# One core, attention, expert mixing and a gated feed-forward: an opening in another order and new step times

## The chip, the cores and the metric

The kernel runs on one core of one Trainium2 chip. The metric is the device time of one launch in microseconds (us); lower is better. The engines are PE (TensorE: matmuls and transposes, with PEld for its weight loads), DVE (VectorE), ACT (ScalarE), POOL (GpSimd) and SP (SyncE), whose queue issues nearly all transfers between DRAM and on-chip memory.

## What is computed

Three layers, one after the other, on 8 batches of 576 tokens with 512 features. Shortened from the reference:

```python
def sm_attn(qq, kk, vv):                 # softmax(scale * qq kk^T) vv
    ...
p_packed = sm_attn(p, k, v)              # 32 packed queries per head, 8 heads
x = sm_attn(q, p_packed, p_packed)       # 576 queries against the 32 packed rows
...
logits = x @ w_gate                      # 4 experts, the best 2 are kept
for e in range(4):
    q, k, v = x @ wq[e], x @ wk[e], x @ wv[e]
    a = softmax(causal(scale * q @ k.T))
    out += weight[e] * (a @ v @ wo[e])
...
x_prev = shift_by_one_token(x)
xk, xr = mu_k * x + (1 - mu_k) * x_prev, mu_r * x + (1 - mu_r) * x_prev
k = np.maximum(xk @ w_k, 0.0)
return sigmoid(xr @ w_r) * (k * k @ w_v)
```

The weights w_k, w_r and w_v arrive as 64-bit floats.

## The kernel before

The work is written as Python generators, one per piece, and each `yield` ends a step. Every step has a number on one time axis (20 units a batch, `U`), and the steps are traced in the order of these numbers. A list scheduler then orders the instructions of each engine, by readiness in its own model and by a priority that a step may carry. What runs on the chip is that fixed order: each engine takes its instructions one after the other and waits where an operand is not there. The constants at the top of the file are the step numbers and priorities.

The pieces that matter here:

- `front(b, g)` is the first attention of batch b for the head group g (two groups of four heads). Its chain is: scores `s1` on PE from `kT` and `pT` (by `eight`), row maximum `mx` on DVE, exp into `a` on ACT, transposes on PE, `aT` on ACT, times `vn` on PE, `pp` on DVE (L291), a transpose on PE (L296), `ppT` on ACT, scores `s2` with `qT` on PE, `st` on DVE (L303), maximum, difference (L308), exp, then `wa` times `ppT` on PE, whose result is split into a rounded part `PWh` (ACT) and a rest `PWl` (DVE, L315); at last `a2` (DVE) with its parts `A2h` and `A2l` (L329). For batch 0 the small steps of this chain run on DVE, later on POOL.
- `values` and `project` multiply `PW` and `A2` on PE into `vg` and into q and k of two experts; two swaps `qs` and `ks` by DMA move halves of them between partitions (L428, L429). `soft`, `turn` and `pair_out` are the second attention: scores (L466), maximum on DVE (L478), exp on ACT (L482), transposes (L505, L512), `tb` on ACT, times `vg` on PE (L548), scaling, and `dt` on POOL, stored to `dscr` (L582).
- `fold` is weight work of no batch: it loads `won` and splits it on POOL into `woTh` and `woTl` (L202, L646), then for each of 24 blocks of w_k and w_r fetches `raw` (128 x 512 words, 256 KB), decodes it (`decode`: `dce`, `dcx`, `dce`, `dcu` on DVE, `dcx` on POOL at L626, `dcq` on ACT, `wc` on DVE at L640), splits it on POOL and multiplies it on PE (L695) into DRAM. It is spread over the attention in 57 steps (`FOLD_T`).
- Behind the attention come the R stage (`rstage`, L854: six blocks of 256 token groups, two halves each; `load_block` fetches `dl` in four parts per block, two blocks fit), the K stage (L874) and the V stage (L915). `swap_w` and `load_weight` bring `wr`, and `swap_end` brings `wk0` and `wk1` (four transfers of 512 KB each) for them.

The transfers of the opening, in SP's order before: pT 64 KB, kT 576, pT 64, kT 576, vn 512 and 64, qT 576 (group 0), vn 512 and 64, qT 576 (group 1), wa 2 x 772, won 512, raw 256, raw 256. Tiles for matmul results are few: two `big` ones and four `one` ones on the chip's accumulator memory.

Of the kernel before, what the change touches and what calls it, by code (L numbers as in the profile page):

```python
# [22 lines left out]

FRONT_T = [-29.55, -25.88, -23.33, -18.77, -17.51, -15.03, -12.67, -12.1, -8.35]
G1_T = [1.16, 2.9, 3.77, 1.72, 1.63, 2.21, 3.77, 1.1, 3.2]
VAL_T = [-2.9, -1.08, -0.99, -0.13, 0.58]
PROJ_T = [-2.12, -1.5, 1.92, 2.48]
GROUPS = ((0, 3), (1, 2), (4,))
SOFT_T = [1.36, 2.42, 3.15]
TURN_LAG = [4.11, 4.87, 5.4]  # L30
OUT_LAG = [3.85, 4.64, 7.81]
FOLD_T = [-20.0, 10.15, 107.63]
FOLD_N = 13
WA_AT = -28.3
PR0, WARM = (1000, 1000, 1000, 1000, 1000, 1000, 940, 980, 980), 16
WR_AT = 6.87
R_LOAD, R_RUN = ([14.0, 15.0], [22.0, 28.0])
W_AT = [1.69, 3.59]
K_AT = [(0, -1.0, 0)] + [(0, 0.0, j) for j in range(4)] + [(1, -1.0, 0)] + [(1, 0.0, j) for j in range(5)]
# [8 lines left out]
E_DT, E_WL = "P", "P"  # L48
PR = {'front': 0, 'values': -100, 'project': 0, 'soft': 0, 'turn': 0, 'out': 100, 'fold': 0, 'k': 0, 'gates': 0}


def f32(ap):
    return ap.bitcast(F32)
# [3 lines left out]
def kernel(  # L57
# [5 lines left out]
    P = 128  # L63
# [77 lines left out]
    if True:  # L141
# [59 lines left out]
        def pool_copy(o, x):  # L201
            nc.gpsimd.tensor_scalar(o, x, 1.0, 0.0, op0=ALU.mult, op1=ALU.add)  # L202

        def evac(eng, o, x):
            if eng == "A":
                nc.scalar.copy(o, x)  # L206
            elif eng == "V":
                nc.vector.tensor_copy(o, x)
            else:
                pool_copy(o, x)  # L210

# [18 lines left out]
        def load(b, gs):  # L230

            for g in gs:
                pT = pTs[(b * NG + g) % 2]
                nc.sync.dma_start(pT, p[b, g].rearrange("d j n -> d (j n)"))
                kT = ld.tile([P, NH, SH], F32, tag="kT", name=nm("kT"))
                nc.sync.dma_start(kT, k[b, g])
                loaded[b, g] = [pT, kT]
            for g in gs:
                vn = vns[(b * NG + g) % 2]
                nc.sync.dma_start(  # L240
                    vn[:, : NT - 1, :], v[b, g, : (NT - 1) * P].rearrange("(c p) x -> p c x", p=P)
                )
                nc.sync.dma_start(vn[TAIL:, NT - 1, :], v[b, g, (NT - 1) * P :])
                qT = ld.tile([P, NH, SH], F32, tag="qT", name=nm("qT"))
                nc.sync.dma_start(qT, q[b, g])
                loaded[b, g] += [vn, qT]

        def front(b, g):
# [33 lines left out]
            for c in range(NT):  # L282
# [7 lines left out]
            pp = fr.tile([P, 2, D], F32, tag="pp", name=nm("pp"))  # L290
            nc.vector.tensor_scalar(  # L291
                pp, ps[:, :D].unsqueeze(1).to_broadcast([P, 2, D]), ri, None, op0=ALU.mult
            )
            yield
            ps = one()
            nc.tensor.transpose(ps[:, :P], pp.rearrange("p x d -> p (x d)"), ident)  # L296
            ppT = fr.tile([P, P], F32, tag="ppT", name=nm("ppT"))
            evac(E_PPT, ppT, ps[:, :P])
# [354 lines left out]
        def fold():  # L655

            won = dv.tile([P, NDT, 2 * P], F32, tag="wc", name=nm("won"), bufs=1)
            nc.sync.dma_start(won, wo.rearrange("(c p) n -> p c n", p=P))  # L660
            woT = {x: dv.tile([P, NDT, 2 * P], F32R, name="woT" + x, bufs=1) for x in "hl"}
# [428 lines left out]
```

## Time and profile before

| | |
|---|---|
| median of 3 runs | 827.92 us (823.35 to 831.87) |
| time of the profiled execution | 830.5 us |
| its span in the trace | 828.7 us |
| mean granted clock of PE | 0.967 of full speed |
| busy in the span: PE, DVE, ACT, POOL | 93%, 59%, 58%, 46% |

The page cuts the span into slices and gives the busy share of each engine in each. A PE that is busy all the time can still run at half clock, which the line PEclk tells. The profiled execution took 830.5 us, of which 828.7 us are the span. In the attention (about 60 to 430 us) and behind it (430 to 828 us) PE is busy nearly throughout; in the first 50 us it is not.

### The profile page before, as it was taken

How to read it: one execution, taken by the hardware profiler on the slowest of the kernel's cores; microseconds unless marked ns; L12 is line 12 of the kernel's file. 1: busy time of each engine (PE TensorE's matmuls, PEld its weight loads, DVE VectorE, ACT ScalarE, POOL GpSimd, SP SyncE). 2: the span in 40 equal slices, each digit the busy share in tenths (PEclk: the TensorE clock that was granted, in tenths of full speed). 3: DMA queues.
4: the chain of work that ended last, by engine and by line, in shares of the span. 5: the costliest groups of instructions: out<-in, count | busy, mean ns of one | idle time of the engine just before them, and what ended most of it. 6: DMA issues, size and time to landing. Idle time of an engine off the chain costs nothing.

```text
span 828.7 us, 15307 instructions
## 1 busy us (share of the span) xinstructions
PE 774.5 (93%) x5504; PEld 623.5 (75%) x5504; DVE 485.7 (59%) x1172; ACT 479.6 (58%) x1093; POOL 380.8 (46%) x490
## 2 busy tenths in 40 slices
PE   5388999999999899989899899999999999999998
PEld 4176877859678596868677778888888888888886
DVE  1979787786868767675764777787584111111111
ACT  2258768677686777787743523242678855565400
POOL 4647757484674735233601236171166343434510
PEclk8579999999999999999999989999999999999999
DMA  9646383564745345112744958586889755555521
GB/s 323 208 137 204 115 229 113 159 182 119 202 123 168 106 126 168 49 49 78 222 146 140 335 205 292 181 275 202 310 281 309 231 170 183 190 152 185 150 66 51
DMA packets 89835, 147.81 MB, mean 178 GB/s; under 512 B 6816, under 2 KB 61600, under 8 KB 87456
## 3 DMA queue, kind: packets, MB, share of 16 engines
q1 hardware_dynamic: 89616, 146.84, 56.1%
q8 instruction: 44, 0.72, 0.4%
q14 instruction: 31, 0.25, 0.1%
q10 hardware_dynamic: 144, 0.00, 0.0%
HBM read 87.04 MB, written 50.33 MB: 166 GB/s over the span
## 4 chain that ended last, share of the span: by engine, by line
PE 68%; DVE 13%; DMA 8%; ACT 6%; issue 2%; POOL 2%; SPq 1%; DVEq 0%; POOLq 0%; ACTq 0%
PE one L915 24%; PE big L874 8%; PE one L874 8%; PE one L548 4%; PE big L407 4%; PE one L854 3%; PE one L352 3%; PE one L695 3%; DVE ms L478 3%; DMA dl<-dscr 3%; ACT ms L482 2%; PE one L466 2%; PE big L854 2%; PE one L505 2%; DMA won<-in_wo_dram 1%
## 5 line engine op out<-in xcount | busy, mean ns | idle before, releaser
L920 DVE TENSOR_TENSOR ring<-one,ring 128x512 f32<-128x512 f32 x36 | 24.9, 692 | 168.8 <-PE one L915 161.4
L915 PE MATMUL one<-wvh,yh 128*128 128x512 f32 x288 | 112.0, 389 | 0.0
L915 PE MATMUL one<-wvl,yh 128*128 128x512 f32 x288 | 112.0, 389 | 0.0
L915 PE MATMUL one<-wvh,yl 128*128 128x512 f32 x288 | 112.0, 389 | 0.0
L482 ACT ACTIVATE ms<-ms,nb 64x64 f32<-64x64 f32 (+4 forms) x160 | 89.5, 560 | 26.1 <-DVE nb L478 24.1
L206 ACT COPY tb<-one 64x128 f32<-64x128 f32 (+5 forms) x208 | 64.0, 354 | 20.3 <-PE one L512 19.4
L548 PE MATMUL one<-tb,vg 128*64 128x320 f32 (+4 forms) x448 | 64.9, 379 | 6.5 <-ACT tb L206 4.3
L626 POOL TENSOR_TENSOR dcx<-dcx,dcu 128x256 f32<-128x256 f32 x40 | 30.6, 765 | 83.7 <-DVE dcu L620 72.0
L213 POOL TENSOR_TENSOR yl<-yvh,yh 128x1024 fp32r<-128x1024 f32 (+1 forms) x24 | 49.1, 2064 | 43.3 <-ACT yh L900 25.5
L478 DVE CUSTOM_DVE_ANT_0 ms<-one,mstrip 64x64 f32<-64x64 f32 (+3 forms) x128 | 51.7, 421 | 18.6 <-PE one L466 16.4
L915 PEld LDWEIGHTS one<-wvh,yl 128*128 128x128 f32 x288 | 54.1, 188 | 11.3
L915 PEld LDWEIGHTS one<-wvl,yh 128*128 128x128 f32 x288 | 54.1, 188 | 11.3
L915 PEld LDWEIGHTS one<-wvh,yh 128*128 128x128 f32 x288 | 54.1, 188 | 11.0
L548 PEld LDWEIGHTS one<-tb,vg 128*64 128x64 f32 x448 | 37.0, 140 | 31.6 <-ACT tb L206 6.9
L505 PE MATMUL one<-ident,ms 128*128 128x128 f32 x320 | 56.0, 284 | 3.9 <-ACT tb L206 2.6
L213 POOL TENSOR_TENSOR yl<-yvl,yh 128x1024 fp32r<-128x1024 f32 x16 | 38.2, 2399 | 41.2 <-ACT yh L900 19.7
L505 PEld LDWEIGHTS one<-ident,ms 128*128 128x128 f32 x320 | 38.2, 142 | 20.8 <-ACT tb L206 7.0
L213 POOL TENSOR_TENSOR dt<-cb 128x192 f32<-128x192 f32 (+1 forms) x48 | 29.9, 652 | 34.8 <-DVE cb L565 18.4
L466 PE MATMUL one<-ks,qs 128*128 128x64 f32 (+3 forms) x128 | 41.7, 350 | 2.3 <-ACT aT L206 0.9
L630 ACT ACTIVATE dcq<-raw 128x256 f32<-128x256 f32 x40 | 17.5, 437 | 42.1 <-DMA raw<-in_w_v_dram 19.2
L466 PE MATMUL one<-kl,qs 128*128 128x64 f32 (+3 forms) x128 | 40.3, 315 | 0.0
L1037 ACT ACTIVATE ring<-ring 128x1024 f32<-128x1024 f32 x18 | 19.1, 1061 | 35.4 <-DMA ring<-rscr 35.4
(206 smaller groups left out, 2084.2 us busy)
## 6 DMA issues: line engine op xcount, KB each, us to landing
yscr<-y SPq DMA_DIRECT2D x48, 384.0 KB, 3.5
dl<-dscr SPq DMA_DIRECT2D x40, 256.0 KB, 5.4
yvh<-yscr SPq DMA_DIRECT2D x10, 1024.0 KB, 5.7
kT<-in_k_dram SPq DMA_DIRECT2D x16, 576.0 KB, 4.5
qT<-in_q_dram SPq DMA_DIRECT2D x16, 576.0 KB, 5.1
rscr<-rr SPq DMA_DIRECT2D x12, 768.0 KB, 4.6
ring<-rscr SPq DMA_DIRECT2D x36, 256.0 KB, 2.9
out_dram<-ring SPq DMA_DIRECT2D x36, 256.0 KB, 3.2
```

Of the source, the lines that this page charges most:

```text
L206: nc.scalar.copy(o, x)
L213: nc.gpsimd.tensor_tensor(o, x, y, op=op)
L407: nc.tensor.matmul(ps[:, 512 * hf : 512 * hf + SH], ww[:, g, :], xx[:, g, :], start=i == 0, stop=i == 3 * NG - 1,)
L466: nc.tensor.matmul(ps[:, po : po + kn], qs[:, i * P : i * P + P], keys[:, ko : ko + kn], start=x == 0, stop=x == 1,)
L478: nc.vector.tensor_tensor_reduce(halves(mv) if last else mv, sv, halves(mk) if last else mk, op0=ALU.add, op1=ALU.min, scale=-SC, scalar=3 ...
L482: nc.scalar.activation(mv, mv, AF.Exp, bias=nb[p0:], scale=-1.0, accum_out=bat["sums"][p0:, i, e : e + 1],)
L505: nc.tensor.transpose(ps[:, at + j * P : at + (j + 1) * P], ms[:, j * P : (j + 1) * P], ident)
L548: nc.tensor.matmul(av[64 * ee : 64 * ee + 64, qo - lo : hi - lo], vg[:, j, HD * (2 * ep + ee) : HD * (2 * ep + ee + 1)], tslice(tabs[ee], ...
L626: nc.gpsimd.tensor_add(f32(t["x"]), f32(t["x"]), f32(t["u"]))
L854: nc.tensor.matmul(po, dx[:, NS * t + s, t0 : t0 + P], wpart("r", s, wx, t), start=n == 0, stop=n == 3 * KT - 1,)
L874: nc.tensor.matmul(po.rearrange("p (b n) -> p b n", b=2), wpart("k0" if f < 4 else "k1", s, wx, t)[:, f % 4 * P : f % 4 * P + P], dx[:, :, ...
L915: nc.tensor.matmul(ps, a[:, f, P * t : P * t + P], wres["v"][b][:, f, :], start=n == 0, stop=n == 3 * NFT - 1,)
```

## The change

Three things. First, SP's order in the opening: `load` for batch 0 now issues `won` and the first two `raw` blocks between the loads of group 0 and those of group 1, where `fold` used to issue them at its own first steps. Second, `decode` of the first four blocks is tied: its first DVE instruction stands behind a chosen instruction of group 0's chain on DVE, and its ACT instruction behind one on ACT (`mark` records them, `behind` adds the order; neither adds a wait on another engine). Third, nearly all step times and some priorities have other numbers; the first 13 fold steps have times of their own, the loads of `wr`, of the R blocks and of `wk0` and `wk1` are moved.

```diff
-FRONT_T = [-29.55, -25.88, -23.33, -18.77, -17.51, -15.03, -12.67, -12.1, -8.35]
-G1_T = [1.16, 2.9, 3.77, 1.72, 1.63, 2.21, 3.77, 1.1, 3.2]
+FRONT_T = [-29.55, -26.81, -23.33, -16.88, -17.51, -14.04, -12.67, -12.1, -8.35]
+G1_T = [1.16, 2.9, 2.88, 1.72, 1.63, 8.09, 3.77, 1.61, 3.2]
...
-WR_AT = 6.87
-R_LOAD, R_RUN = ([14.0, 15.0], [22.0, 28.0])
-W_AT = [1.69, 3.59]
+WR_AT = 7.97
+R_LOAD, R_RUN = ([15.94, 16.11], [22.78, 27.99])
+W_AT = [4.54, 4.03]
...
             for g in gs:
+                if b == 0 and g == 1:
+                    first["won"] = dv.tile([P, NDT, 2 * P], F32, tag="wc", name=nm("won"), bufs=1)
+                    nc.sync.dma_start(first["won"], wo.rearrange("(c p) n -> p c n", p=P))
+                    first["raw"] = [fetch_raw(w_k, c * P, 0) for c in range(2)]
...
+        def mark(b, g, eng, x, ins):
+
+            if b == 0 and g == 0:
+                for turn in {"V": [(0,), (1,), (2, 3)], "A": [(0, 1), (2, 3)]}[eng][x]:
+                    first[eng, turn] = ins.ins
...
+        def behind(ins):
+            return tc.issue_after(ins) if ins is not None else nullcontext()
...
-            nc.vector.tensor_scalar(
-                t["e"], hi, 3, 0x3FFFFFF8, op0=ALU.logical_shift_left, op1=ALU.bitwise_and
-            )
+            with behind(first["V", turn] if turn is not None else None):
+                nc.vector.tensor_scalar(
+                    t["e"], hi, 3, 0x3FFFFFF8, op0=ALU.logical_shift_left, op1=ALU.bitwise_and
+                )
...
-                    decode(wc[:, c, :], src, c * P, f0)
+                    decode(wc[:, c, :], src, c * P, f0, first["raw"].pop(0) if first["raw"] else None, c if f0 == 0 and m == 0 else None)
...
-        add("fold", fold(), even(FOLD_T[0], FOLD_T[1], FOLD_N) + even(FOLD_T[1], FOLD_T[2], NFOLD - FOLD_N))
+        add("fold", fold(), FOLD_0 + even(FOLD_T[0], FOLD_T[1], NFOLD - len(FOLD_0)))
```

In the order rows below a row has its place on the engine, its line, its operation, result and operands with running numbers, and the shape; xN stands for N alike in a row. Lines behind the first edit are higher in the changed file (L291 is L300 there, L303 is L312, L611 is L624, L640 is L654, L761 is L774).

The first place is DVE in the opening, from the `pp` of group 0 on. Before (raw_313 is the first weight block, st_303 the scores of group 0, pp_284 the `pp` of group 1):

```order
16 L291 TENSOR_SCALAR pp_253<-one_232,ri_15_191 128x128
17 L271 RECIPROCAL ri_23_218<-su_22_215 128x1
18 L611 TENSOR_SCALAR dce_316<-raw_313 128x256
19 L614 SCALAR_TENSOR_TENSOR dcx_315<-raw_313,dce_316 128x256
20 L617 TENSOR_SCALAR dce_316<-dcx_315 128x256
21 L620 SCALAR_TENSOR_TENSOR dcu_317<-raw_313,dce_316 128x256
22 L611 TENSOR_SCALAR dce_375<-raw_372 128x256
23 L303 STREAM_TRANSPOSE st_303<-big_294 128x288 x2
24 L291 TENSOR_SCALAR pp_284<-one_263,ri_23_218 128x128
```

The same place on DVE after the change (raw_172 is the first weight block, pp_292 the `pp` of group 1, st_307 the scores of group 0):

```order
17 L300 TENSOR_SCALAR pp_261<-one_240,ri_18_197 128x128
18 L624 TENSOR_SCALAR dce_329<-raw_172 128x256
19 L627 SCALAR_TENSOR_TENSOR dcx_328<-raw_172,dce_329 128x256
20 L630 TENSOR_SCALAR dce_329<-dcx_328 128x256
21 L633 SCALAR_TENSOR_TENSOR dcu_330<-raw_172,dce_329 128x256
22 L300 TENSOR_SCALAR pp_292<-one_271,ri_24_216 128x128
23 L654 SCALAR_TENSOR_TENSOR wc_325<-dcq_331,dcx_328 128x256
24 L312 STREAM_TRANSPOSE st_307<-big_298 128x288 x2
```

The first decode still stands ahead of group 0's `st`; the `pp` of group 1 has moved ahead of it, the start of the second decode behind it, and the first `wc`, which needs POOL, ahead of it.

The second place is SP's queue in batch 7, where the R weights, the last swaps and the first R blocks are issued. Before:

```order
192 L761 DMA wrl_5634<-wscrr 128x1024 x4
193 L428 DMA qs_113<-l_5837 64x576
194 L429 DMA qs_113<-l_5837 64x576
195 L428 DMA ks_5876<-ks_5876 64x576
196 L429 DMA ks_5876<-ks_5876 64x576
197 L761 DMA dl_5636<-dscr 128x2x256 x4
198 L582 DMA dscr<-dt_5937 128x4x192
199 L761 DMA dl_5636<-dscr 128x2x256 x4
```

SP's queue at the same place after the change:

```order
192 L774 DMA wrl_5634<-wscrr 128x1024 x4
193 L437 DMA qs_113<-l_5857 64x576
194 L438 DMA qs_113<-l_5857 64x576
195 L437 DMA ks_5884<-ks_5884 64x576
196 L438 DMA ks_5884<-ks_5884 64x576
197 L591 DMA dscr<-dt_5935 128x4x192
198 L774 DMA dl_5636<-dscr 128x2x256 x8
```

The first R block no longer follows the swaps at once; it stands behind a store of `dt`, with the second block.

The third place is SP's queue in the R stage, where `wk0` and `wk1` are fetched among the R blocks (`dl`). Before:

```order
211 L761 DMA dl_5636<-dscr 128x2x256
212 L864 DMA rscr<-rr_6454 128x1536
213 L761 DMA wk0l_6382<-wscrk_84 128x1024 x4
214 L761 DMA wk1l_6408<-wscrk_85 128x1024 x4
215 L864 DMA rscr<-rr_6488 128x1536
216 L761 DMA dl_5636<-dscr 128x2x256 x3
217 L864 DMA rscr<-rr_6544 128x1536
218 L761 DMA dl_5636<-dscr 128x2x256 x3
```

SP's queue at the same place after the change:

```order
209 L774 DMA dl_5636<-dscr 128x2x256
210 L774 DMA wk0l_6406<-wscrk_84 128x1024 x4
211 L877 DMA rscr<-rr_6440 128x1536
212 L774 DMA dl_5636<-dscr 128x2x256 x3
213 L774 DMA wk1l_6500<-wscrk_85 128x1024 x4
214 L877 DMA rscr<-rr_6476 128x1536
215 L774 DMA dl_5636<-dscr 128x2x256
216 L877 DMA rscr<-rr_6536 128x1536
```

The rest of the fifth R block (three parts) now stands between `wk0` and `wk1`; before, its last two parts stood behind both.

## Rows read from the trace of the kernel before

**Rows 1.** Busy time by stretch: us, then each engine's busy us, granted clock, DMA share, GB/s.
```profile
0.00:10.00 10.00, 6.27 (x48) 5.63 (x49) 2.25 (x11) 2.32 (x4) 8.76 (x33) 1.00 0.79 262
10.00:20.00 10.00, 5.38 (x123) 3.04 (x123) 1.62 (x7) 2.38 (x5) 0.00 (x0) 0.78 1.05 379
...
30.00:40.00 10.00, 4.50 (x37) 1.70 (x37) 10.00 (x21) 3.19 (x5) 4.17 (x5) 0.50 0.43 115
...
200.00:300.00 100.00, 95.32 (x962) 74.67 (x961) 75.34 (x233) 73.90 (x215) 61.81 (x103) 0.98 0.51 148
...
500.00:600.00 100.00, 100.00 (x443) 82.84 (x442) 73.86 (x114) 37.58 (x68) 39.24 (x40) 1.00 0.75 249
```

**Rows 2.** Instructions in order of time, DVE in the opening: start, us, and idle before.
```profile
13.48 0.34 DVE L291 TENSOR_SCALAR pp<-one,ri 128x128 f32<-128x128 f32 x1
...
21.96 0.30 DVE L611 TENSOR_SCALAR dce<-raw 128x256 int32<-128x256 int32 x1 [8.07 <-DMA raw<-in_w_k_dram]
...
24.72 0.83 DVE L303 STREAM_TRANSPOSE st<-big 128x288 f32<-128x288 f32 x2
25.48 0.30 DVE L291 TENSOR_SCALAR pp<-one,ri 128x128 f32<-128x128 f32 x1
```

**Rows 3.** The same view, PE in the opening.
```profile
15.61 1.21 PE L222 MATMUL big<-qT,ppT 64*32 64x288 f32 x16
...
25.84 0.48 PE L296 MATMUL one<-ident,pp 128*128 128x128 f32 x1 [8.45 <-DVE pp L291]
```

**Rows 4.** The same view, POOL in the opening.
```profile
21.34 1.72 POOL L202 TENSOR_SCALAR woTh<-won 128x256 fp32r<-128x256 f32 x4 [11.48 <-DMA won<-in_wo_dram]
...
23.03 3.03 POOL L646 TENSOR_TENSOR woTl<-won,woTh 128x256 fp32r<-128x256 f32 x4
...
26.02 0.72 POOL L626 TENSOR_TENSOR dcx<-dcx,dcu 128x256 f32<-128x256 f32 x1
```

**Rows 5.** The same view, issues of SP in the opening.
```profile
9.38 0.38 SPq L660 DMA_DIRECT2D won<-in_wo_dram  x1
9.80 1.63 SPq L761 DMA_DIRECT2D raw<-in_w_k_dram  x2
```

**Rows 6.** The same view, the end of the opening.
```profile
44.55 1.09 DVE L329 TENSOR_TENSOR A2l<-a,A2h 128x576 fp32r<-128x576 f32 x1
...
58.83 0.27 PE L466 MATMUL one<-ks,qs 128*128 128x64 f32 x1 [0.95 <-ACT aT L206]
```

**Rows 7.** The same view, SP and PE in the R stage.
```profile
458.85 3.19 SPq L761 DMA_DIRECT2D wk0l<-wscrk  x4
...
462.14 2.74 SPq L761 DMA_DIRECT2D wk1l<-wscrk  x4
...
475.29 0.73 PE L854 MATMUL big<-wrh,dh 128*128 128x512 f32 x2 [2.16 <-DVE rr L839]
...
478.26 1.22 PE L854 MATMUL one<-wrh,dh 128*128 128x512 f32 x2 [0.99 <-ACT dh L823]
```

**Rows 8.** Busy time by stretch, columns as in the first group: behind two waits.
```profile
404.00:408.00 4.00, 4.00 (x22) 3.80 (x21) 1.73 (x9) 2.77 (x9) 4.00 (x7) 0.59 0.85 255
...
460.00:480.00 20.00, 16.85 (x68) 13.06 (x68) 13.75 (x14) 12.46 (x15) 7.66 (x3) 0.91 1.01 372
480.00:500.00 20.00, 20.00 (x83) 16.34 (x83) 16.28 (x18) 3.65 (x7) 2.98 (x2) 0.92 0.49 188
```

**Rows 9.** Instructions in order of time, SP and PE in batch 7.
```profile
397.26 0.46 SPq L429 DMA_DIRECT2D ks<-ks  x1
397.78 4.13 SPq L761 DMA_DIRECT2D dl<-dscr  x4
...
403.43 0.37 PE L466 MATMUL big<-ks,qs 128*128 128x288 f32 x1 [1.96 <-DMA ks<-ks]
```

**Rows 10.** The same view, PE: two long waits between 60 and 430 us.
```profile
280.98 4.50 PE L548 MATMUL one<-tb,vg 128*64 128x256 f32 x24 [2.26 <-ACT tb L206]
...
373.34 3.47 PE L548 MATMUL one<-tb,vg 128*64 128x320 f32 x16 [2.04 <-ACT tb L206]
```

More of the change, by code (lines that the diff above doesn't have):

```diff
@@ L1 @@
 import math
-from contextlib import ExitStack
+from contextlib import ExitStack, nullcontext
 import concourse.bass as bass
@@ L20 @@
 EPS = 1e-9
-FRONT_T = [-29.55, -25.88, -23.33, -18.77, -17.51, -15.03, -12.67, -12.1, -8.35]
-G1_T = [1.16, 2.9, 3.77, 1.72, 1.63, 2.21, 3.77, 1.1, 3.2]
-VAL_T = [-2.9, -1.08, -0.99, -0.13, 0.58]
-PROJ_T = [-2.12, -1.5, 1.92, 2.48]
+FRONT_T = [-29.55, -26.81, -23.33, -16.88, -17.51, -14.04, -12.67, -12.1, -8.35]
+G1_T = [1.16, 2.9, 2.88, 1.72, 1.63, 8.09, 3.77, 1.61, 3.2]
+VAL_T = [-2.96, -0.14, -0.55, -0.02, 0.48]
+PROJ_T = [-1.9, -1.68, 2.14, 2.7]
 GROUPS = ((0, 3), (1, 2), (4,))
[L29 to L35, printed above, removed]
-WR_AT = 6.87
-R_LOAD, R_RUN = ([14.0, 15.0], [22.0, 28.0])
-W_AT = [1.69, 3.59]
+SOFT_T = [1.76, 1.61, 2.48]
+TURN_LAG = [4.11, 4.69, 5.4]
+OUT_LAG = [3.59, 4.38, 7.43]
+FOLD_0 = [-21.87, -18.2, -16.87, -12.45, -10.56, -6.17, -3.87, -1.87, -0.37, 1.63, 3.63, 7.17, 8.98]
+FOLD_T = [5.65, 105.86]
+WA_AT = -30.0
+PR0, WARM = (1000, 985, 1043, 1073, 1000, 1000, 940, 980, 907), 16
+WR_AT = 7.97
+R_LOAD, R_RUN = ([15.94, 16.11], [22.78, 27.99])
+W_AT = [4.54, 4.03]
 K_AT = [(0, -1.0, 0)] + [(0, 0.0, j) for j in range(4)] + [(1, -1.0, 0)] + [(1, 0.0, j) for j in range(5)]
@@ L48 @@
 E_DT, E_WL = "P", "P"
-PR = {'front': 0, 'values': -100, 'project': 0, 'soft': 0, 'turn': 0, 'out': 100, 'fold': 0, 'k': 0, 'gates': 0}
+PR = {'front': 0, 'values': -100, 'project': 0, 'soft': 0, 'turn': 0, 'out': 100, 'fold': 0, 'k': 46, 'gates': 0}
 def f32(ap):
@@ L205, in evac @@
             if eng == "A":
[L206 to L210, printed above, removed]
+                return nc.scalar.copy(o, x)
+            if eng == "V":
+                return nc.vector.tensor_copy(o, x)
+            pool_copy(o, x)
         def pool_tt(o, x, y, op):
@@ L290, in front @@
             pp = fr.tile([P, 2, D], F32, tag="pp", name=nm("pp"))
-            nc.vector.tensor_scalar(
+            mark(b, g, "V", 0, nc.vector.tensor_scalar(
                 pp, ps[:, :D].unsqueeze(1).to_broadcast([P, 2, D]), ri, None, op0=ALU.mult
-            )
+            ))
             yield
@@ L297, in front @@
             ppT = fr.tile([P, P], F32, tag="ppT", name=nm("ppT"))
-            evac(E_PPT, ppT, ps[:, :P])
+            mark(b, g, "A", 0, evac(E_PPT, ppT, ps[:, :P]))
             yield
@@ L307, in front @@
             small = nc.gpsimd if b else nc.vector
-            small.tensor_tensor(
+            mark(b, g, "V", 1, small.tensor_tensor(
                 st3, st3, m2.unsqueeze(2).to_broadcast([P, NCB, NPK]), op=ALU.subtract
-            )
-            nc.scalar.activation(st, st, AF.Exp, scale=SC)
+            ))
+            mark(b, g, "A", 1, nc.scalar.activation(st, st, AF.Exp, scale=SC))
             yield
@@ L326, in front @@
             a2 = fr.tile([P, S], F32, tag="sa", name=nm("a2"), bufs=4)
-            nc.vector.transpose(a2, st)
+            mark(b, g, "V", 2, nc.vector.transpose(a2, st))
             evac("P" if b else "A", bat["A2h"][:, g, :], a2)
@@ L596, in fetch_raw, with decode @@
             return raw
-        def decode(dst, src, r0, f0, raw=None):
+        def behind(ins):
+            return tc.issue_after(ins) if ins is not None else nullcontext()
+        def decode(dst, src, r0, f0, raw=None, turn=None):
             if src.dtype != I64:
@@ L610, in decode @@
             }
-            nc.vector.tensor_scalar(
-                t["e"], hi, 3, 0x3FFFFFF8, op0=ALU.logical_shift_left, op1=ALU.bitwise_and
-            )
+            with behind(first["V", turn] if turn is not None else None):
+                nc.vector.tensor_scalar(
+                    t["e"], hi, 3, 0x3FFFFFF8, op0=ALU.logical_shift_left, op1=ALU.bitwise_and
+                )
             nc.vector.scalar_tensor_tensor(
@@ L629, in decode @@
             if E_SQ == "A":
-                nc.scalar.activation(f32(t["q"]), f32(hi), AF.Square)
+                with behind(first["A", turn] if turn is not None else None):
+                    nc.scalar.activation(f32(t["q"]), f32(hi), AF.Square)
             else:
@@ L655, in fold @@
         def fold():
-            won = dv.tile([P, NDT, 2 * P], F32, tag="wc", name=nm("won"), bufs=1)
-            nc.sync.dma_start(won, wo.rearrange("(c p) n -> p c n", p=P))
+            won = first["won"]
             woT = {x: dv.tile([P, NDT, 2 * P], F32R, name="woT" + x, bufs=1) for x in "hl"}
@@ L736, in call @@
             yield
-        bats, loaded = {}, {}
+        bats, loaded, first = {}, {}, {}
         steps = []
@@ L936 @@
         add("front", zeros(), [-6.0 + 0.5 * i for i in range(7)])
-        add("fold", fold(), even(FOLD_T[0], FOLD_T[1], FOLD_N) + even(FOLD_T[1], FOLD_T[2], NFOLD - FOLD_N))
-        swap = max(last, FOLD_T[2] + 0.1)
+        add("fold", fold(), FOLD_0 + even(FOLD_T[0], FOLD_T[1], NFOLD - len(FOLD_0)))
+        swap = max(last, FOLD_T[1] + 0.1)
         add("k", call(swap_w), [swap])
```

## The prediction

> **What bounds the kernel now.** I read the summary by slices first: PE is busy nearly throughout, except in the first 50 us. The table by stretches says the same in numbers: 95.32 of 100 us at a clock of 0.98 in the middle of the attention, 100 of 100 at 1.00 behind it, but 4.50 of 10 us at 0.50 between 30 and 40 us, where DVE is busy 10.00 of 10 [rows 1]. PE has the same matmuls in both kernels, and the order of instructions shows that; so the change can win only by idle or half-clock time of PE. There are three kinds of it: the opening, where DVE sets the pace; a handful of waits of about 2 us in the attention; and one place in the R stage. I then read each of them in the list of instructions with what ended the idle time before them, and the chain of waits, which in the opening goes through the load of `won`, the POOL split, `wc` and on through DVE.
>
> The opening in steps. The first `pp` ends at 13.8 us, and then DVE waits 8.07 us for `raw`, whose decode stands next in its queue [rows 2]. The first `s2` on PE is through at about 16.8 (15.61 + 1.21) [rows 3], so `st` could start there, but it stands behind the decode and starts at 24.72; the `pp` of group 1 follows at 25.48 [rows 2], and PE idles 8.45 us for it [rows 3]. About 8 us of the opening are thus a transfer that stands late in its queue: `won` and the two `raw` are issued at 9.38 and 9.80, last of all [rows 5].
>
> **The opening.** I sum what each transfer has ahead of it, itself included, in SP's order. Before: `won` 5,640 KB, `raw` 5,896. After: `won` 2,944, first `raw` 3,200, second 3,456, the last piece of group 1's `vn` 4,032 (before: 3,008). At 262 GB/s in the first 10 us (2,559 KB) and 379 GB/s from then on (370 KB a us) [rows 1], `raw` comes before at 10 + 3,337/370 = 19.0; it came at 21.96 [rows 2], 3 us later than its bytes, and `won` at 21.34 against 18.3 [rows 4], also 3 us later. After, bytes alone give `won` 11.1, `raw` 11.7, `vn` 14.0; with 3 us on top 14.0, 14.7, 17.0. I take 12.9, 13.5 and 15.5: fewer transfers are in flight together at that moment, so less than the full 3 us, but not none.
>
> The moved `wc` needs POOL's `dcx`, which stands behind the split of `won`: the split runs from 21.34 to 26.02, 4.68 us, and `dcx` takes 0.72 [rows 4]. So after: 12.9 + 4.68 + 0.72 = 18.3, `wc` about 0.43 (from the decode's other DVE steps, which take 0.3 to 0.8 [rows 2]), and `st` at 18.8, between 17.0 (all by bytes, bounded by `s2`) and 19.9. Against 24.72 that is 5.9 us earlier (4.8 to 7.7). The `raw` wait goes, and what is late next is POOL's split. The transfers of group 1 behind `won` and `raw` cost nothing by this: `vn` at 15.5 is before `st`, and the `pp` of group 1, at 25.48 before, has some 8 us of room.
>
> From `st` to the last `A2l` (44.55, 1.09 long [rows 6]) DVE is full [rows 1], so the count of its instructions decides: 40 before, 15 of them decode, and 36 after, 11 of them decode. Four decode steps of some 0.5 us are 2 us, but some of them only move to where DVE has room and others lie on POOL's pace; I take 0.6 us, at most 1.4. PE's work behind that is the same up to the first score of the second attention at 58.83 [rows 6] (5 PE rows fewer stand ahead of it, which must be done later and gain nothing). Sum of the opening: **−6.5 us**, from −4 to −8.
>
> On the landing of transfers a rule speaks. The rows show `raw` 3 us later than its bytes [rows 2]. The Trainium skill, DMA: Bandwidth & Descriptors, section "Queues, rings and completion order", says that each DMA engine consumes descriptors in ring order, but that completion is not first-in-first-out for an issuing engine. By ring order alone, an estimate from that page's rule, the bytes ahead would decide, `st` would come at 17.0 and the total would be about 2 us lower than mine; the late landing here is what the rule leaves room for by its second half.
>
> **The R stage.** `wk0` and `wk1`, 2 MB each, are issued at 458.85 and 462.14 ahead of the last parts of the fifth R block; PE waits 2.16 us and 0.99 us at 475.29 and 478.26 [rows 7], the releasers being the shift work on the block. The granted clock is 0.91 and 0.92 in the two stretches of 20 us around it [rows 8], 3.4 us of full-speed work short; the 3.15 us of waiting at half clock would be 1.6 of these, which leaves 1.8 of slow work. So at most 5.0 us can go. After, the rest of that block has only `wk0` ahead: 2,048 + 768 KB at 249 GB/s ([rows 1], a stretch of steady transfers; 243 KB a us) is 11.6 us, against some 15 us of R work that PE still has at that point (pairs of matmuls in the order, at 0.45 us from start to start). The next block has `wk1` ahead too and needs about 24 us, against about 25 that PE works until it. So the waits should go, the second of them just: **−4.5 us**, 0 if the block is late anyway.
>
> **Batch 7.** PE waits 1.96 us at 403.43 for the swap `ks`, issued at 397.26, and the first R block of four transfers follows it from 397.78 and shares the queue [rows 9]; the next 4 us run at 0.59 of the clock, 1.6 us lost [rows 8]. At most 3.6 us can go. After, the R block is behind a store of `dt` and the swap has the queue to itself; but the PE work between `project` and the scores that wait for `ks` falls from about 8.8 to 6.6 us (counted in the order with the durations of the trace of before), and the swap with its copies needs nearly that. I take less than half: **−1.5 us**, 0 to −3.6.
>
> **Steady state.** Seven batches are retimed, and no row of before tells what the new order waits for. I compared how much PE work lies between a producer and its user. Better: between `project` and the first score at least 3.9 us instead of 2.7. Worse: between the `vn` matmul (L284) and the `pp` transpose (L296) a median of 1.6 us instead of 4.7, only the s2 and `wa` matmuls of one group. For bounds I use the longest present waits between 60 and 430 us, 2.26 and 2.04 us [rows 10]. All waits there together are 95.32 against 100 [rows 1], so about 18 us over the attention; a quarter more or less is 4.5. I take **0**, ±4.5.
>
> Sum: 830.5 − 6.5 − 4.5 − 1.5 + 0 = 818.0 us for the profiled execution. That one was 0.3% above the median of 827.92 (830.5), so the forecast is 818.0 × 827.92/830.5 = 815.5, rounded to **816 us**. One per cent, 8.3 us, is about what a measurement of this kernel can tell from no change: faster means below 819.6, slower above 836.2.
>
> **Rivals.**
> (a) The opening's wait changes its name: POOL's split of `won` is late or DVE behind it is no shorter. If the transfers keep their 3 us and the split is slowed by DVE's work beside it, `st` comes at 21 to 22 and the opening gains 3 instead of 6.5: 821.5, scaled 819, with a spread to 821. For it: POOL stands on the chain of waits now [rows 4]. Against: its start moves with `won`.
> (b) The R block is late anyway, since its cover is only as long as the transfer: 822.5, scaled 820.
> (c) The steady state takes back 5 to 18 us without deciding the sign: 821 to 836.
> (d) Slower. The place is `pp`: DVE must normalise it between the `vn` matmul and its transpose on PE, and only 1.6 us of PE work are left there. If DVE has another instruction in hand each time, PE waits as it does at its longest waits now, 2.26 and 2.04 us [rows 10], and what follows such a wait runs slow, as 404 to 408 us do [rows 8]: 1.6 to 1.8 us more. That is 3.9 us a batch, 27 in seven, and the time would be 843. It eats the gain of 12.5 from 1.8 us a batch and is slower by over 1% from about 3 us a batch. For it: 4.7 to 1.6 us is a large cut, and DVE is busy three quarters of the time there (75.34 of 100 us [rows 1]). Against: the chain itself, a DVE step of 0.34 us [rows 2], fits into 1.6 us, if DVE is free.
> (e) The steady state gains by its longer covers before the scores, 5 to 12 us: 803 to 811.
>
> **How the numbers follow.** The forecast (811 to 820.5) has 0.48, of which 0.43 lies below 819.6; (a) 0.14, of which 0.05 below; (b) 0.12, of which 0.01; (c) 0.08, all within 1%; (d) 0.06; (e) 0.12. Faster by over 1%: 0.43 + 0.05 + 0.01 + 0.12 = 0.61; within: 0.33; slower: 0.06. The range of 806 to 828 leaves out part of (e), the upper half of (c) and all of (d), some 0.16 together.
>
> **What would show it.** Right: no DVE wait for `raw` of more than 1 to 2 us, `st` of group 0 between 17 and 20 us, the first score of batch 0 at 51 to 54 us instead of 58.83; no PE wait near the fifth and sixth R block and a clock of 0.98 or more there; no wait for `ks` in batch 7. Wrong: DVE's `wc` waiting for POOL until 21 or later, PE waiting for `dh` or `rr` in the R stage, waits of 2 us for DVE's `pp` in most batches. The prediction fails most easily in the steady state, where I have put nothing.

## The result and the profile after

The changed kernel takes 803.17 us (median of 6 runs, 801.48 to 804.62) against 826.97 for the kernel before in the same hours; the ratio is 0.9707, interval 0.9675 to 0.9738. That is 24 us, about twice the 11 to 12 us of the forecast, and outside its range of 806 to 828. The two profiled executions lie further apart (830.5 and 801.5 us), so the traces have 29 us to explain where the medians have 24.

The page of after, its head and the slices of PE; then busy time by stretch (columns as in [rows 1]):

```profile
span 799.7 us, 15316 instructions
...
PE 754.7 (94%) x5504; PEld 617.7 (77%) x5504; DVE 489.6 (61%) x1172; ACT 476.8 (60%) x1093; POOL 387.5 (48%) x490
...
PE   6788979899899999989899999999999999999998
...
PEclk8599999999999999999999999999999999999999
```

```profile
0.00:20.00 20.00, 12.11 (x172) 9.14 (x172) 7.79 (x26) 5.68 (x12) 15.23 (x44) 0.89 0.92 317
20.00:40.00 20.00, 14.68 (x115) 8.99 (x116) 19.18 (x46) 7.78 (x16) 7.49 (x11) 0.51 0.87 295
40.00:60.00 20.00, 17.59 (x219) 16.27 (x218) 14.99 (x50) 12.85 (x34) 11.50 (x20) 1.00 0.54 141
60.00:420.00 360.00, 335.61 (x3337) 274.42 (x3335) 281.14 (x820) 272.79 (x802) 207.35 (x322) 0.99 0.48 145
420.00:795.00 375.00, 373.83 (x1665) 308.49 (x1665) 165.81 (x232) 177.71 (x232) 145.95 (x95) 1.00 0.64 214
```

The same stretches of before:

```profile
0.00:20.00 20.00, 11.65 (x171) 8.67 (x171) 3.86 (x17) 4.70 (x9) 8.76 (x33) 0.89 0.92 321
20.00:40.00 20.00, 7.99 (x71) 2.84 (x71) 17.49 (x35) 5.02 (x9) 11.74 (x17) 0.50 0.69 215
40.00:60.00 20.00, 16.16 (x146) 14.33 (x147) 13.84 (x34) 9.19 (x21) 10.53 (x17) 0.76 0.47 137
60.00:420.00 360.00, 338.00 (x3342) 268.47 (x3341) 274.16 (x834) 269.67 (x794) 202.09 (x323) 0.98 0.49 140
420.00:824.00 404.00, 399.72 (x1775) 328.74 (x1774) 175.69 (x254) 191.00 (x263) 147.71 (x100) 0.99 0.62 207
```

To see where the 29 us went, I cut both spans into stretches of 5 us and took from each PE's idle time (5 less busy) and its half-clock loss (busy times 1 less the granted clock). What is left of the span is PE's work at full clock. The last stretch ends with the span, 3.7 and 4.7 us long, and PE is mostly idle in it.

| us | before: idle + clock loss | after |
|---|---|---|
| 0 to 60 | 24.2 + 8.5 | 15.6 + 8.3 |
| 60 to 420 | 22.0 + 6.1 | 24.4 + 2.9 |
| behind 420, without the last stretch | 4.3 + 2.9 | 1.2 + 0.0 |
| whole span | 54.3 + 17.5 | 44.9 + 11.3 |
| work at full clock | 756.9 | 743.5 |

Idle time gave 9.4 us and the clock 6.2, together what the prediction was looking for. The other 13.4 us are time that PE no longer needs for its work, though both kernels have the same 5504 matmuls. One line has most of it, the second attention's `tb` times `vg`. Its group on the page of before and of after:

```profile
L548 PE MATMUL one<-tb,vg 128*64 128x320 f32 (+4 forms) x448 | 64.9, 379 | 6.5 <-ACT tb L206 4.3
```

```profile
L557 PE MATMUL one<-tb,vg 128*64 128x320 f32 (+4 forms) x448 | 54.1, 366 | 2.4 <-DVE nb L487 1.4
```

Busy time falls by 10.8 us with the count unchanged, and the mean of one only from 379 to 366 ns. From each row's start to the next (idle time taken out) they take 62.5 us before and 52.4 after; with each row weighted by the clock granted to it, 59.3 and 51.3, so 8.0 of the 13.4 us are this line's. The rows of the group overlap in time, so less overlap makes the group longer at the same mean.

The 448 rows are 16 sets of 28. What one set looks like on PE, before:

```profile
161.14 0.75 PE L548 MATMUL one<-tb,vg 128*64 128x320 f32 x2
161.82 0.77 PE L558 MATMUL big<-ident,cx 128*128 128x128 f32 x5
162.52 0.72 PE L222 MATMUL big<-qT,ppT 64*32 64x288 f32 x16
163.16 0.87 PE L548 MATMUL one<-tb,vg 128*64 128x256 f32 x8
163.97 0.33 PE L296 MATMUL one<-ident,pp 128*128 128x128 f32 x1
```

After:

```profile
204.40 3.08 PE L557 MATMUL one<-tb,vg 128*64 128x320 f32 x28
207.41 0.77 PE L567 MATMUL big<-ident,cx 128*128 128x128 f32 x5
```

Each matmul of the code is two rows in the profile (14 of the code, 28 here). A set alternates between two halves, `tb` of one expert for output partitions 0 to 63 and of the other for 64 to 127. Before, the first matmul of one half stands alone (x2, 0.68 us to the next start), four follow at 163.16 (0.81), and the other nine at 164.22 take 2.20: 3.69 us. After, the uncut set takes 3.01, and others take 2.85. The lone matmul has a tenth of the set's columns (320 of 3200); one after the other, ten such would take up to 6.8 us by this estimate, so the matmuls of a whole set must overlap. My reading is that a matmul without its mate of the other half beside it takes its time alone; the experiments test it. In PE's order 15 of 16 sets of before have such a lone matmul (a run of rows whose number of matmuls is odd), 6 of after.

The opening, DVE in order of time, answering to [rows 2] and [rows 6]:

```profile
13.65 0.40 DVE L624 TENSOR_SCALAR dce<-raw 128x256 int32<-128x256 int32 x1 [0.69 <-DMA raw<-in_w_k_dram]
...
17.92 0.35 DVE L300 TENSOR_SCALAR pp<-one,ri 128x128 f32<-128x128 f32 x1 [1.75 <-PE one L293]
18.18 0.41 DVE L654 SCALAR_TENSOR_TENSOR wc<-dcq,dcx 128x256 f32<-128x256 f32 x1
19.11 0.85 DVE L312 STREAM_TRANSPOSE st<-big 128x288 f32<-128x288 f32 x2 [0.51 <-PE big L221]
...
35.23 0.74 DVE L338 TENSOR_TENSOR A2l<-a,A2h 128x576 fp32r<-128x576 f32 x1
```

POOL answering to [rows 4], and PE, where group 1's `vn` is waited for and where the first score of the second attention stands:

```profile
12.76 1.54 POOL L202 TENSOR_SCALAR woTh<-won 128x256 fp32r<-128x256 f32 x4 [2.92 <-DMA won<-in_wo_dram]
14.27 3.16 POOL L660 TENSOR_TENSOR woTl<-won,woTh 128x256 fp32r<-128x256 f32 x4
17.39 0.72 POOL L639 TENSOR_TENSOR dcx<-dcx,dcu 128x256 f32<-128x256 f32 x1
```

```profile
16.57 1.29 PE L293 MATMUL one<-vn,aT 128*32 128x64 f32 x40 [3.22 <-DMA vn<-in_v_dram]
...
46.50 0.33 PE L475 MATMUL one<-ks,qs 128*128 128x192 f32 x1
```

The 8.07 us for `raw` [rows 2] are 0.69, `st` starts at 19.11 instead of 24.72, the last `A2l` at 35.23 instead of 44.55, the first score at 46.50 instead of 58.83 (other work has moved across that point, so 12.3 is not the gain; the table's 8.8 is).

In the R stage one wait of PE stands in place of two [rows 7], and the clock stays full [rows 8]:

```profile
459.71 0.73 PE L867 MATMUL one<-wrh,dh 128*128 128x512 f32 x2 [1.17 <-ACT dh L836]
```

```profile
440.00:460.00 20.00, 18.83 (x83) 15.31 (x82) 15.44 (x17) 11.55 (x16) 8.97 (x4) 1.00 0.98 381
460.00:480.00 20.00, 20.00 (x89) 16.52 (x89) 15.10 (x16) 5.39 (x10) 5.73 (x4) 1.00 0.68 238
```

### The profile page after: what moved, and what is told of

It reads as the page before. It is cut to its first block, busy times and chain, and to the rows that moved or that the text cites. A ratio compares the mean times of both kernels' runs of the same rounds, so it can differ in the third digit from the quotient of the medians.

```text
span 799.7 us, 15316 instructions
## 1 busy us (share of the span) xinstructions
PE 754.7 (94%) x5504; PEld 617.7 (77%) x5504; DVE 489.6 (61%) x1172; ACT 476.8 (60%) x1093; POOL 387.5 (48%) x490
## 4 chain that ended last, share of the span: by engine, by line
PE 67%; DVE 16%; ACT 7%; DMA 4%; issue 3%; POOL 2%; SPq 0%; DVEq 0%; POOLq 0%; ACTq 0%
PE one L928 24%; PE one L887 8%; PE big L887 8%; PE one L867 4%; PE big L867 4%; PE one L557 4%; PE one L708 3%; ACT ms L491 3%; PE big L416 3%; DVE ms L487 3%; PE one L361 2%; PE one L514 1%; DVE kl L435 1%; PE one L475 1%; DMA vn<-in_v_dram 1%
## 5 line engine op out<-in xcount | busy, mean ns | idle before, releaser
L491 ACT ACTIVATE ms<-ms,nb 128x192 f32<-128x192 f32 (+4 forms) x160 | 89.3, 559 | 26.4 <-DVE nb L487 24.1
L206 ACT COPY tb<-one 64x128 f32<-64x128 f32 (+5 forms) x208 | 62.1, 362 | 6.2 <-PE one L521 4.4
L928 PEld LDWEIGHTS one<-wvh,yl 128*128 128x128 f32 x288 | 54.1, 188 | 11.3
L928 PEld LDWEIGHTS one<-wvl,yh 128*128 128x128 f32 x288 | 54.1, 188 | 11.1
L487 DVE CUSTOM_DVE_ANT_0 ms<-one,mstrip 128x192 f32<-128x192 f32 (+3 forms) x128 | 51.6, 422 | 10.1 <-PE one L475 7.6
L557 PE MATMUL one<-tb,vg 128*64 128x320 f32 (+4 forms) x448 | 54.1, 366 | 2.4 <-DVE nb L487 1.4
L514 PE MATMUL one<-ident,ms 128*128 128x128 f32 x320 | 49.3, 276 | 7.3 <-ACT ms L491 6.3
L557 PEld LDWEIGHTS one<-tb,vg 128*64 128x64 f32 x448 | 32.6, 138 | 22.9 <-issue 4.0
L1050 ACT ACTIVATE ring<-ring 128x1024 f32<-128x1024 f32 x18 | 19.1, 1060 | 35.1 <-DMA ring<-rscr 35.1
L475 PE MATMUL one<-ks,qs 128*128 128x192 f32 (+3 forms) x128 | 38.6, 328 | 0.0
L475 PE MATMUL one<-kl,qs 128*128 128x192 f32 (+3 forms) x128 | 38.2, 309 | 0.0
L660 POOL TENSOR_TENSOR wl<-wc,wh 128x256 fp32r<-128x256 f32 x48 | 35.5, 758 | 0.4
```

What stands on the lines that cost most here:

```text
L206: return nc.scalar.copy(o, x)
L475: nc.tensor.matmul(ps[:, po : po + kn], qs[:, i * P : i * P + P], keys[:, ko : ko + kn], start=x == 0, stop=x == 1,)
L487: nc.vector.tensor_tensor_reduce(halves(mv) if last else mv, sv, halves(mk) if last else mk, op0=ALU.add, op1=ALU.min, scale=-SC, scalar=3 ...
L491: nc.scalar.activation(mv, mv, AF.Exp, bias=nb[p0:], scale=-1.0, accum_out=bat["sums"][p0:, i, e : e + 1],)
L514: nc.tensor.transpose(ps[:, at + j * P : at + (j + 1) * P], ms[:, j * P : (j + 1) * P], ident)
L557: nc.tensor.matmul(av[64 * ee : 64 * ee + 64, qo - lo : hi - lo], vg[:, j, HD * (2 * ep + ee) : HD * (2 * ep + ee + 1)], tslice(tabs[ee], ...
```

## The experiments

Each run was timed beside the kernel before in the same hours. The ratio is to that, with its 95% interval in brackets, and gains in us are taken from the ratio, on 827 us.

**Parts of the change, by its constants.** The code of before or after, with the named constants from the other file.

`opening_only` (after, with the old `FRONT_T` to `OUT_LAG`, `WR_AT`, `R_LOAD`, `R_RUN`, `W_AT`, `PR`):

> The changed opening (early won and raw, the tie, the first fold steps and priorities) with every other step time and priority of before. If the two traces are read rightly, the idle and half-clock time of PE in the first 60 us falls from 32.7 to 23.9 us: about 9 us faster than before, 818 us. If the late raw was the only cost, as the prediction had it, 6.5 us: 820.5. If the gain of the opening is given back later, 824 or more.

820.36 us, ratio 0.9915 (0.9889 to 0.9940): 7.0 us, near the 6.5 of the prediction. In its trace idle and clock loss of the first 60 us are 21.8 us against 32.7 before, 10.9 less, while PE's work at full clock is 3.3 us more; so the 7.0 are a balance.

`steady_only` (before, with this and the like):

```diff
-FRONT_T = [-29.55, -25.88, -23.33, -18.77, -17.51, -15.03, -12.67, -12.1, -8.35]
+FRONT_T = [-29.55, -26.81, -23.33, -16.88, -17.51, -14.04, -12.67, -12.1, -8.35]
...
-OUT_LAG = [3.85, 4.64, 7.81]
+OUT_LAG = [3.59, 4.38, 7.43]
```

> Before, with only the step times of the attention (front, values, project, soft, turn, out) new. Theory of the pairs (the two column halves of tb x vg run side by side on PE only where their matmuls alternate in its queue; the new times break them less often, 25 runs of L548 instead of 41): 7 to 12 us faster, 815 to 820, and the time of L548 from start to next start falls from 62.5 to 50 to 54 us. Rival (L548 is shorter in the trace of after only because its clock was full more of the time; the steady state gives nothing, as the prediction had it): 823 to 831.

810.75 us, ratio 0.9812 (0.9785 to 0.9839): 15.5 us, more than either theory. `tb` times `vg` takes 55.4 us. Two things come out of its trace. First, PE's work at full clock is 746.6 us, 10.3 less than before, while its waits in 60 to 420 us are no shorter (26.1 + 6.4). Second, its opening is better too: idle and clock loss of the first 60 us are 26.7 against 32.7, because the new front times have already put the first decode behind the `st` of group 0 on DVE.

`r_only` (before, with `WR_AT`, `R_LOAD`, `R_RUN`, `W_AT`, `PR` of after):

> Before, with only the loads of wr, of the R blocks and of wk0 and wk1 moved, and the priority of the K stage. Idle and half-clock time behind 430 us falls by 4.6 us in the two traces: 822 us. If the waits are another transfer's or come back, within 1.5 us of before.

821.90 us, ratio 0.9932 (0.9907 to 0.9956): 5.6 us. The moved loads do what was forecast for them.

`no_opening` (before, with the constants of both of these):

> Before, with the new step times of the attention and the moved loads of the weights and R blocks, but the opening of before (won and raw issued last, no tie, old fold steps and priorities): all of the change but its first two parts. If the gains of the parts add up as the single runs gave them (16.6 and 5.4), 805.5, and the new opening is worth only the 2 us that are left to the 803 of the whole, since the new step times already put the first decode behind the st of group 0. If the opening's 7 us add to the rest, 810.

807.57 us, ratio 0.9750 (0.9723 to 0.9778), against 0.9707 for the whole change: the new opening adds 3.6 us to the rest, between the two expectations. DVE in its opening:

```profile
15.36 0.85 DVE L303 STREAM_TRANSPOSE st<-big 128x288 f32<-128x288 f32 x2 [0.34 <-PE big L222]
...
21.66 0.29 DVE L611 TENSOR_SCALAR dce<-raw 128x256 int32<-128x256 int32 x1 [3.88 <-DMA raw<-in_w_k_dram]
```

`raw` is as late as before and still waited for, but `st` is ahead of it, at 15.36. Idle and clock loss of the first 60 us are 27.3 us here, 32.7 before and 23.9 after: of the 8.8 us, 5.4 are won by order alone. The parts alone give 7.0 + 15.5 + 5.6 = 28 where the whole gives 24; the overlap is this opening.

`front_only` (before, with `FRONT_T` and `G1_T` of after) and `soft_only` (with `SOFT_T`, `TURN_LAG`, `OUT_LAG` of after):

> Before, with only the times of the first attention (front, group 1) new. In DVE's order the first decode moves behind the st of both... of group 0, so that the wait of 8 us for raw no longer holds back the chain: 6 us. 31 runs of L548 instead of 41 at 0.5 us: 5 us. Together 11 us, 816; if the pieces are nothing, 821; if the steady state pays for the late second front, 823 or more.

> Before, with only the times of the second attention (soft, turn, out) new. The opening on DVE stays as before. 35 runs of L548 instead of 41: 3 us faster, 824; with the 5 us that the steady step times gave beyond the opening and the front's share, 822. If nothing here matters, 826 to 829.

823.64 (0.9967, 0.9949 to 0.9984) and 827.22 (1.0012, 0.9993 to 1.0031). Both missed: 2.7 us and nothing. Counting runs of L548 was the wrong count. Lone matmuls go better with the time of the sets: 14 and 13 sets have one in these two kernels, 15 in before, against 8 in `steady_only`. But the sets alone don't explain the misses, as they take 60.2 and 57.8 us here, less than the 62.5 of before. The traces show where that was lost again: in other matmuls that use a part of the array. In `soft_only` the 16 rows of `wa` times `ppT` are cut in five batches; before has all of them whole.

```profile
120.67 0.81 PE L222 MATMUL big<-wa,ppT 64*32 64x386 f32 x2
121.41 0.30 PE L466 MATMUL one<-ks,qs 128*128 128x64 f32 x1
...
122.24 0.87 PE L222 MATMUL big<-wa,ppT 64*32 64x386 f32 x14
123.04 0.66 PE L505 MATMUL one<-ident,ms 128*128 128x128 f32 x4
```

The two pieces take 0.74 and 0.80 us to the next start, a whole group 0.81. The line grows from 15.0 to 18.3 us from start to start, and five times 0.73 is about this. In `front_only` it is `vn` times `aT`, cut in ten places (12.1 to 14.9 us), and `qT` times `ppT`, in five (12.2 to 13.8). In `steady_only` and in after none of these groups is cut behind 60 us. So each table alone moves the cuts to another group. No run took these cuts out, and the new times of `values` and `project`, which `steady_only` has besides, were not tried alone.

**The sets themselves.** `before_pairs` writes the halves in the other order, so that no set of it has a lone matmul in PE's order:

```diff
-                    for ee in range(2):
+                    for ee in (1, 0):
                         nc.tensor.matmul(
```

> Before, with the two halves of each tb x vg step written in the other order (half 1, then half 0), so that the first matmul is not ready before its mate; in PE's order all sets then alternate (22 runs, none with a lone first matmul). Theory of the pairs: 16 sets at 2.85 us, the time of an unbroken set in the trace of after, are 46 us against 62.5: 10 to 16 us faster, 811 to 817. Rival (clock, not order): within 4 us of before.

836.03 us, ratio 1.0114 (1.0090 to 1.0138): slower by 9. The set now waits, as its first matmul needs the later `tb`:

```profile
L548 PE MATMUL one<-tb,vg 128*64 128x320 f32 (+4 forms) x448 | 59.6, 421 | 13.9 <-ACT tb L206 13.8
```

```profile
184.03 4.62 PE L548 MATMUL one<-tb,vg 128*64 128x320 f32 x28 [2.08 <-ACT tb L206]
```

Waits of the line are 13.9 us instead of 6.5, and sets behind a wait run partly at half clock (4.55 us to the next start against 2.86 for one at full clock). PE's work at full clock did fall, from 756.9 to 747.0 us. So the expected 10 us were there, and 14.2 us more idle time ate them (the traces are 4.6 us apart): before, a lone matmul was what PE did while it waited for the second `tb`.

`after_broken` writes the order that before had on PE, inside one set:

```diff
+            todo = todo[:1] + todo[10:] + todo[1:10]
+            for av, lo, hi, nj, j, ee in todo:
```

> After, with the 14 matmuls of each tb x vg set written in the order in which before had them on PE: the first of half 0 for queries 256 to 575, then the set for queries 0 to 255, then the rest; 15 of the 16 sets then break the alternation of the halves once, where 8 did. Theory of the pairs: a broken set takes 3.6 us against 2.85, so about 7 x 0.75 = 5 us slower than after, 808. Rival (a set's time is its number of matmuls, the rest was the clock): 801 to 805.

806.55 us, ratio 0.9737 (0.9709 to 0.9766): 2.5 us slower than after's 0.9707, with overlapping intervals. The sets take 53.8 us, 1.4 more, not 5. An uncut set in this order takes 3.01 us against 2.85, so the halves still overlap inside a run. The order inside the run was not the cost; what is left as the cost is a lone matmul at the end of a run (6 sets have one here, as in after).

`after_apart` writes all of half 0 and then all of half 1:

```diff
-                for j in range(nj):
-                    qo = max(lo, j * P)
-                    for ee in range(2):
+                for ee in range(2):
+                    for j in range(nj):
+                        qo = max(lo, j * P)
```

> After, with each tb x vg set written half by half (all of half 0, then all of half 1), so that few matmuls have one of the other half beside them. If two halves run side by side on PE, as the theory of the pairs has it, a set grows from 2.85 to some 5.3 us: 16 x 2.5 = 40 us slower, 843. If the matmuls run one by one anyway, within 4 us of after.

829.89 us, ratio 1.0021 (1.0003 to 1.0040): 26 us slower than after. Its sets:

```profile
263.62 4.59 PE L557 MATMUL one<-tb,vg 128*64 128x320 f32 x28
```

4.53 us to the next start against 2.85, and 81.1 us over all sets against 52.4. The two halves do run side by side, and the order alone is worth as much as the whole change. Whether the matmuls themselves overlap or the weight loads between them was not separated. Its size was overestimated, 28.7 for 40.

`sets_whole` and `sets_cut` tie PE's order in a set, each part behind the part before it. Both also issue the set's `cx` transposes one step earlier than after does, so they compare cleanly with each other, and less so with after:

```diff
+            for part in ((QB, S), (0, QB), "cx"):
+                with tc.issue_after(prev) if prev is not None else nullcontext():
```

for `sets_whole`, and for `sets_cut`

```diff
+            for part in ((QB, S), "cx", (0, QB)):
+                with tc.issue_after(prev) if prev is not None else nullcontext():
```

> After, with PE's order tied in each tb x vg set: queries 256 to 575, queries 0 to 255, then the five cx transposes; 17 uninterrupted runs of L548's matmuls on PE instead of 26. Theory of the pieces (a set costs PE some 0.5 us more for each time that its run is cut by other work; the order of the halves inside a run costs 0.16 us at most): the sets take 46 to 49 us from start to next start instead of 52.4; unless the tie makes PE wait for tb, 4 to 6 us faster than after, 798. Rival (only a run that waits is longer): 801 to 806.

> The same kernel with the five cx transposes tied between the two parts of each set: 34 runs instead of 17, the same matmuls in the same alternation. Theory of the pieces: 17 more cuts at 0.4 to 0.5 us, 7 to 8 us slower than the uncut one in the same call, and the sets take 54 to 57 us. Theory of the alternation alone: the same time as uncut within 2 us.

799.12 (0.9669, 0.9645 to 0.9692) and 806.60 (0.9768, 0.9744 to 0.9792): the uncut one is some 4 us faster than after (the two intervals overlap slightly), the cut one 7.5 slower than the uncut, both as expected. The first has 1 set with a lone matmul in PE's order and 17 runs, the second 2 and 34. The line's sets take 49.9 and 55.3 us. A set in each, and in the first one whose first matmul stands alone since the second `tb` is late:

```profile
200.76 2.93 PE L566 MATMUL one<-tb,vg 128*64 128x320 f32 x28
203.62 0.77 PE L556 MATMUL big<-ident,cx 128*128 128x128 f32 x5
...
349.89 0.72 PE L566 MATMUL one<-tb,vg 128*64 128x320 f32 x2 [1.09 <-DVE nb L487]
351.15 2.92 PE L566 MATMUL one<-tb,vg 128*64 128x320 f32 x26 [0.54 <-ACT tb L206]
```

```profile
201.20 2.27 PE L566 MATMUL one<-tb,vg 128*64 128x320 f32 x20
203.40 0.77 PE L556 MATMUL big<-ident,cx 128*128 128x128 f32 x5
204.10 0.87 PE L566 MATMUL one<-tb,vg 128*64 128x256 f32 x8
```

A cut between two full pairs costs 2.20 + 0.80 - 2.86 = 0.14 us; a lone first matmul costs 0.72 + 2.85 - 2.86 = 0.7. Seventeen cuts are thus 2.4 of the 5.4 us, and 1.4 more are slow clock in the sets; the `cx` transposes take 1.5 us more (9.6 and 11.1). The rest was not taken apart. The total came as expected, with a price per cut that was too high.

**The opening's two halves.** `after_late_raw` issues `won` and both `raw` behind group 1's loads:

```diff
-                if b == 0 and g == 1:
-                    first["won"] = dv.tile([P, NDT, 2 * P], F32, tag="wc", name=nm("won"), bufs=1)
...
                 loaded[b, g] += [vn, qT]
+                if b == 0 and g == 1:
+                    first["won"] = dv.tile([P, NDT, 2 * P], F32, tag="wc", name=nm("won"), bufs=1)
...
```

> After, with won and the first two raw blocks issued behind group 1's loads (ahead of wa) instead of ahead of them; the tie and all times as after. By the prediction, raw is 1.1 MB later in the queue, about 3 us, and the first decode stands ahead of st of group 0: 2 to 3 us slower than after, 806. Rival (group 1's vn, which after waits for, comes earlier and pays for it): 801 to 804.

804.64 us, ratio 0.9725 (0.9698 to 0.9752): 1.5 us slower than after, with overlapping intervals. The trace has the late `raw`: DVE waits 5.11 us for it, `st` starts at 21.30, and idle and clock loss of the first 60 us are 26.8 us against 23.9. The times neither confirm these 2.9 us nor exclude them.

`after_no_tie` leaves the order of the decode to the scheduler:

```diff
-            return tc.issue_after(ins) if ins is not None else nullcontext()
+            return nullcontext()
```

> After without the tie: won and raw are early, but the scheduler is free to put the decodes where its model has them ready, and on DVE it puts the first decode ahead of group 0's pp and the second one ahead of its st. By the prediction's reading of the opening (what stands ahead of st on DVE sets the pace), the chain waits for raw and one more decode: 3 to 5 us slower than after, 807. If early transfers alone make the opening, 801 to 805.

800.61 us, ratio 0.9669 (0.9644 to 0.9694): not slower, by the ratios 3 us faster (the intervals overlap). `st` starts at 21.33, 2.2 us later than with the tie, but idle and clock loss of the first 60 us are 24.8 us against 23.9: the decodes that stand ahead of `st` no longer stand behind it. The reading that what stands ahead of `st` on DVE sets the whole opening fell here.

> The changed kernel itself, timed beside the next run: 801 to 805. What the run without the tie gained (2.6 us on other chips' hours) is only real if this one stays above 802.

> After with uncut tb x vg sets and without the tie of the decode. If the tie costs 2 to 3 us by itself and the cuts 4, 796 to 798, the fastest of all; if the tie's loss was chance, 798 to 800 as with the tie.

803.20 (0.9700, 0.9680 to 0.9719) and 799.20 (0.9653, 0.9632 to 0.9675). With uncut sets the tie makes no difference (799.12 with it). The fastest version is after with uncut sets, 4 us below it (these last two were timed in the same hours, and their intervals are apart).

## Why the prediction was wrong

**What bounds the kernel: the step that failed.** "PE has the same matmuls in both kernels ... so the change can win only by idle or half-clock time of PE." Equal matmuls are not equal time. Two 64-column halves share PE when they alternate (2.85 us a set against 4.53), and a matmul without its mate costs 0.7 us more. The order of before showed the sets cut in three with a lone first matmul, and [rows 10] even point at the line; I read only the waits in them. 13.4 us of the 29 in the traces are busy time that is gone, which the prediction had put at nothing; by the runs, `after_apart` shows the overlap (the Trainium skill, TensorEngine Tiling (Array Packing), section "Tiling Modes", says that different tiles of the array can run matmuls in parallel, and the trace agrees: 2.85 against 4.53 us; I had not asked what the order does to it), `sets_whole` and `sets_cut` its price, `steady_only` that the new times bring it. The sets have 8.0 of the 13.4 us; 9 fewer lone matmuls at 0.7 and 15 fewer cuts at 0.14 are 8.4. The scores (L466) have fewer runs too, 94 and 61, and take 3.9 us less from start to start; that this is the same effect was not tried.

**Steady state, "0, ±4.5".** Measured: 15.5 us alone, of which 6.0 are its share in the opening by the traces; the rest is of the size of that work (10.3). The waits, on which the term was bounded, stayed (28.1 us of idle and clock loss against 27.3). Rival (e), its gain of 5 to 12 us, came true, by another mechanism than longer covers. Rival (d) occurred once, in batch 2, at about its price (a wait of 2.93 us and 1.4 us of clock loss in the 5 us behind it); batch 1 has such a wait of 0.86 us, the batches behind have none:

```profile
104.23 0.42 PE L305 MATMUL one<-ident,pp 128*128 128x128 f32 x1 [2.93 <-DVE pp L300]
```

**Opening, -6.5.** Alone 7.0 us; in the trace of the whole 8.8. That 7.0 is so near is in part luck, as it is what is left of 10.9. Landings forecast 12.9, 13.5 and 15.5 for `won`, `raw` and `vn` came at 12.8, 13.6 and 16.6; `st` forecast at 18.8 came at 19.1, released not by POOL's `wc` but by `s2` on PE, behind group 1's `vn`. The transfers of group 1 were thus not free. From `st` to the last `A2l` DVE took 16.1 us instead of 19.8, 3.7 less where I took 0.6. What the term missed is that the new front times reach much of the same end without early transfers (`no_opening`), so inside the whole change it is worth 3.6. Rival (a) did not occur. By ring order alone (the Trainium skill, DMA: Bandwidth & Descriptors, "Queues, rings and completion order") `raw` would have come at 11.7 and `vn` at 14.0; they came 2 and 2.6 us later. The section's second half, that completion is not first-in-first-out, leaves room for that; no run shows the reason.

**R stage and batch 7, -4.5 and -1.5.** Right: 5.6 us together in `r_only`. The `ks` wait is gone, and one R wait of 1.17 us is left, so rival (b) occurred only in part.

**Sum.** 6.0 for the loads and 6.5 for the opening, less the overlap, were right in kind; the missing 12 us are the steady state.

## What to carry to other kernels

Before a change of order is costed by waits, sum the busy time of each group: where matmuls use parts of the array side by side, as column halves do here, the order decides the busy time (26 us in `after_apart`), and a lone one shows as a run of odd length in the order and as a short row of its own in the trace. Look at all such groups, since a retiming that mends one can cut another (`soft_only`). Repairing the order is only worth it when the operands are there: whole sets cost 9 us in before, where `tb` was late, and gained 4 us in after, where it mostly was not. Parts of a retiming that reach the same wait are not additive; take each out of the whole as well as putting it alone into the kernel before.

## What the runs showed that was not expected

Twenty-eight matmul rows of 64 output columns took 2.85 us in alternation and 4.53 half after half, with nothing else changed. A cut between full pairs cost 0.14 us, a cut behind one lone matmul 0.7, and it was much the same, 0.73, in a group of another tile shape (64 rows by 32 columns, `wa` times `ppT`).
